# Routed attention and MLP: two raw weight buffers in the memory of the MLP's weight sums, loaded two chunks ahead

## The chip, the cores and the metric

The kernel runs on one core of a Trainium2 chip. A core has five engines that run their own instruction streams[...]: TensorE (PE in the profile; its weight loads are PEld), VectorE (DVE), ScalarE (ACT), GpSimd (POOL) and SyncE (SP), which here does nothing but issue transfers. POOL issues transfers too. The metric is the device time of one launch in microseconds (us); the kernel before was timed three times, and its median is what the change is measured against. The trace is of one further execution.

## The reference, cut to what matters

The inputs are four batches of eight heads, 768 positions and 64 channels. Queries and keys are each assigned to the nearest of 16 centroids of their head; a query sees only the keys of its own cluster. The attention output, with its heads side by side, goes through a layer norm and a two-layer MLP with a residual.

```python
q_assign = np.argmax(np.einsum('bhsd,hcd->bhsc', q_n, c_n), axis=-1)
k_assign = np.argmax(np.einsum('bhsd,hcd->bhsc', k_n, c_n), axis=-1)
mask = q_assign[:, :, :, None] == k_assign[:, :, None, :]
scores = np.where(mask, scale * np.matmul(q, k.transpose(0, 1, 3, 2)), -1000000000.0)
attn = softmax(scores)                       # over the keys
x = (attn @ v), heads side by side           # (4, 768, 512)
xn = (x - mu) / np.sqrt(var + 1e-06) * g_ln
out = x + np.maximum(xn @ w_ch1, 0.0) @ w_ch2   # w_ch1 512x2048, w_ch2 2048x512
```

The two weight matrices arrive as 64-bit floats. [...] the kernel turns them into 32-bit floats itself, in 32 chunks of 128 by 512 numbers (512 KB each as it is loaded), by integer arithmetic on the two 32-bit words of each number.

## The kernel before

The attention stage goes through 16 pairs of heads, n = 0 to 15. Each pair has two slots, one for each half of its queries. The conversion of weight chunks is threaded through this stage: one chunk in each slot of pairs 0 to 6 (14 chunks), one in the first slot only of pairs 7 to 14 (8 chunks). The last 10 chunks are converted in the first part of the MLP.

```python
LOAD AND CONVERSION OF A CHUNK (line numbers of the kernel before)
limit = [NWC, 1]                                                   # 219; [1] is the number of buffers
def load_weight(m):                                                # 229
    if m < NWC and m < limit[0]:
        raw = pools["conv"].tile([P, WC], mybir.dt.int64, tag="raw", name="raw", bufs=limit[1])
        nc.sync.dma_start(out=raw, in_=weight_chunk(m)[0])         # 234, issued by SP
        raws[m] = raw

def split_weight(m):        # reads the high words of raw: three DVE operations, L243, L246, L249
    hi = words[:, :, 1]
    ta = pools["conv"].tile([P, WC], U32, tag="ta", name="ta")
    tb = pools["conv"].tile([P, WC], U32, tag="tb", name="tb", bufs=2)
    ...
def join_weight(m):         # three DVE operations, L258, L262, L263; L263 is the last that reads raw
    ...
    nc.vector.scalar_tensor_tensor(                                # 263
        out=fb, in0=lo, scalar=2.0 ** -52, in1=fb, op0=ALU.mult, op1=ALU.mult)
    nc.gpsimd.dma_start(out=w, in_=fb, accum_op=ALU.add)           # 266, issued by POOL, adds into w
...
TWO SETS OF WEIGHT SUMS, used in the MLP only (tag "ws", two buffers of 4 KB in each partition)
def w1_sums(b, j, which=range(4)):                                 # 592
    if 0 in which:
        t = xpool.tile([P, 4, NDH, P], F32, tag="ws", name="ws", bufs=2)
...
THE ATTENTION STAGE; within an engine the order is that of the code
    load_weight(0)                                                 # 674
    for u in range(len(pairs) * slots):                            # 676
        n, slot = divmod(u, slots)
        if slot == 0 and nxt:
            for side in (1, 0):
                prep_transpose(n + 1, side)       # DVE L275, twice: keys and queries of the next pair
                load(n + 2, "qk"[side])           # SP, four transfers each, rows of 128 bytes
        for i in own: scores(i)                   # PE L392 and ACT exp L388, six steps
        if slot == 0:
            if n and nxt: finish(n - 1, 0)        # PE L453, ACT L461, POOL: flat L463, rdens L464
            if nxt: prep_sims(n + 1)              # PE L297, needs both L275 of this slot
        elif nxt:
            prep_onehot(n + 1)                    # PE L339, needs DVE L324
            prep_mask(n + 1, 0); prep_mask(n + 1, 1)
        if slot and n > 1 and nxt:
            finish(n - 2, 2); finish(n - 2, 3)    # DVE L486 or L490, L498; SP stores x_d L501
        if m is not None: split_weight(m)
        for i in own: weigh(i)                    # PE L404, 12 products
        add_up(n, slot, (0,))                     # DVE L436: sums of four exps
        if slot and n and nxt: finish(n - 1, 1)   # DVE L468, POOL: row L470, rb L478
        if nxt: add_up(n, slot, (1,))             # DVE L439, L441
        if m is not None:
            join_weight(m)
            load_weight(m + 1)                    # SP; waits for L263
        if slot == 0:
            load(n + 1, "v")
            if nxt: prep_turn(n + 1); prep_route(n + 1)   # PE L313; DVE L322, L324
        ...                                       # layer norm of batch 0, from pair 6 on
```

The exps have four buffers of two steps each (tag "e"), of which one slot fills three; the scores have three PSUM buffers.

Of the kernel before, what the change touches and what calls it, by code (L numbers as in the profile page):

```python
# [8 lines left out]
F32 = mybir.dt.float32  # L9
# [10 lines left out]
def kernel(  # L20
# [15 lines left out]
    P = 128  # L36
# [14 lines left out]
    xpool = ctx.enter_context(tc.tile_pool(name="xpool", bufs=1))  # L51
# [4 lines left out]
    def pool(name, bufs, **kw):  # L56
        return stage.enter_context(tc.tile_pool(name=name, bufs=bufs, **kw))
# [4 lines left out]
    conv = pool("conv", 1)  # L62
# [5 lines left out]
    pools = {"t": pool("ps_t", 1, space=PSUM), "conv": conv}  # L68
# [22 lines left out]
    def load(n, names):  # L91
        if n >= len(pairs):
            return
        b, pr = pairs[n]
        for name in names:

            if n and name != "v":
                load_blocks(n, name)
                continue
            shape = [P, 2, NT, D] if name == "v" else [P, NT, 2, D]  # L100
            t = loads.tile(
                shape, F32, tag=name, name=f"{name}_sb", bufs=2 if name == "v" else 1
            )

            parts = 1 if n or name == "v" else NHALF
            for g in range(parts):
                cs = slice(g * NT // parts, (g + 1) * NT // parts)
                for j in range(2):
                    queue = nc.scalar if parts > 1 and j else nc.sync
                    queue.dma_start(  # L110
                        out=t[:, j] if name == "v" else t[:, cs, j, :],
                        in_={"q": q, "k": k, "v": v}[name][b, 2 * pr + j].rearrange(
                            "(p c) d -> p c d", p=P
                        )[:, cs, :],
                    )
            loaded[n][name] = t
# [51 lines left out]
    def norm_centroids(part):  # L168
        if part == 0:
            nc.vector.tensor_tensor(c_sq, c_sb, c_sb, ALU.mult)  # L170
            nc.vector.tensor_reduce(c_ss, c_sq, AX.X, ALU.add)

            nc.vector.tensor_scalar_max(c_ss, c_ss, 2.0 ** -100)
        elif part == 1:
            nc.scalar.activation(c_nrm, c_ss, AF.Sqrt)
        else:

            nc.vector.reciprocal(c_tmp, c_nrm)
            nc.vector.scalar_tensor_tensor(
                out=c_tmp, in0=c_tmp, scalar=c_ss, in1=c_nrm, op0=ALU.mult, op1=ALU.add  # L180
            )
            nc.vector.tensor_scalar(c_nrm, c_tmp, 0.5, 1e-6, op0=ALU.mult, op1=ALU.add)
            nc.vector.reciprocal(c_tmp, c_nrm)
            nc.vector.tensor_scalar_mul(c_sb, c_sb, c_tmp)
# [5 lines left out]
    def turn_centroids():  # L190
        ct_ps = ps("ct_ps")
        nc.tensor.transpose(ct_ps[:D, : H * NCL], c_sb, ident[: H * NCL, : H * NCL])
        ct_v = ct_ps[:D, : H * NCL].rearrange("p (r j c) -> p r j c", j=2, c=NCL)
        for j in range(2):
            nc.vector.tensor_copy(cT[j * D : (j + 1) * D, :, j, :], ct_v[:, :, j, :])
# [10 lines left out]
    NDH, NFH = NDC // 2, NFC // 2  # L206
# [7 lines left out]
    WC = 512  # L214
    NW1 = NDC * FF // WC
    NWC = NW1 + NFC
    raws = {}
    halves = {}
    limit = [NWC, 1]

    def weight_chunk(m):
        if m < NW1:
            o, c = divmod(m, NDC)
            cols = slice(o * WC, (o + 1) * WC)
            return moe_w_ch1[c * P : (c + 1) * P, cols], w1[:, c, cols]
        c = m - NW1
        return moe_w_ch2[c * P : (c + 1) * P, :], w2[:, c, :]

    def load_weight(m):
        if m < NWC and m < limit[0]:  # L230
            raw = pools["conv"].tile(
                [P, WC], mybir.dt.int64, tag="raw", name="raw", bufs=limit[1]
            )
            nc.sync.dma_start(out=raw, in_=weight_chunk(m)[0])
            raws[m] = raw

# [34 lines left out]
    def prep_transpose(n, side):  # L271
        src = loaded[n]["qk"[side]]
        t_sb = prepared[n][side] = heads.tile([P, S], F32, tag=f"t{side}", name=f"t{side}")
        if n:
            nc.vector.transpose(t_sb, src)  # L275
            return
        for g in range(NHALF):
            t = ps_s.tile([P, 2, 512], F32, tag="s", name="qk_ps")[:, 0]
            for c in range(TH):
                nc.tensor.transpose(  # L280
                    t[:, c * P : (c + 1) * P],
                    src[:, g * TH + c, :, :].rearrange("p h d -> p (h d)"),
                    ident,
                )
            if side == 0 or g == 1:
                nc.scalar.copy(t_sb[:, g * HC : (g + 1) * HC], t[:, :HC])
            else:
                nc.vector.tensor_copy(t_sb[:, g * HC : (g + 1) * HC], t[:, :HC])
# [351 lines left out]
    with tc.manual_schedule(engines=order | {mybir.EngineType.SP}):  # L640

        idle = ps_a.tile([P, 512], F32, tag="a", name="idle_ps")

        def busy(m):
            for _ in range(m):
                nc.tensor.matmul(idle[:, :P], zeros, zeros, start=True, stop=True)

        busy(26)
        norm_centroids(0)
        prep_transpose(0, 0)  # L650
        load(1, "q")
        load(0, "v")
        norm_centroids(1)
        norm_centroids(2)
        busy(4)
        prep_transpose(0, 1)
        load(1, "k")
        busy(8)
        turn_centroids()
        busy(8)  # L660
        nc.scalar.activation(warm, warm, AF.Exp, scale=0.0)
        prep_sims(0)
        busy(10)
        prep_turn(0)
        scores(0, "qk", ("qk",))
        prep_route(0)
        prep_onehot(0)
        prep_mask(0, 0)
        prep_mask(0, 1)
        for i in range(1, AHEAD):  # L670
            scores(i, "qk", ("qk",))
        for i in range(AHEAD):
            scores(i, "qk", ("mask", "exp"))
        load_weight(0)
    with tc.manual_schedule(engines=order | {mybir.EngineType.Pool}):
        for u in range(len(pairs) * slots):
            n, slot = divmod(u, slots)
            nxt = n + 1 < len(pairs)
            own = range(GROUP * u, GROUP * (u + 1))
            if slot == 0 and not nxt:  # L680
                finish(n - 1, 0)
            if slot == 0 and nxt:
                for side in (1, 0):
                    prep_transpose(n + 1, side)
                    load(n + 2, "qk"[side])
            for i in own:
                if i >= AHEAD:
                    scores(i)
            if slot == 0:
                if n and nxt:  # L690
                    finish(n - 1, 0)
                if nxt:
                    prep_sims(n + 1)
            elif nxt:
                prep_onehot(n + 1)
                prep_mask(n + 1, 0)
                prep_mask(n + 1, 1)
            for job in extra.pop((n, f"between {slot}"), ()):
                job()
            if slot and n > 1 and nxt:  # L700
                finish(n - 2, 2)
                finish(n - 2, 3)
            m = convert.get((n, slot))
            if m is not None:
                split_weight(m)
            for i in own:
                weigh(i)
            add_up(n, slot, (0,))
            if slot and n and nxt:
                finish(n - 1, 1)  # L710
            if nxt:
                add_up(n, slot, (1,))
            if m is not None:
                join_weight(m)
                load_weight(m + 1)
            if slot == 0:
                load(n + 1, "v")
                if nxt:
                    prep_turn(n + 1)
                    prep_route(n + 1)  # L720
                else:
                    for part in (2, 3):
                        finish(n - 2, part)
                    finish(n - 1, 1)
            elif not nxt:
                for part in (2, 3):
                    finish(n - 1, part)
            for job in extra.pop((n, slot), ()):
                job()
# [25 lines left out]
    hid = pool("hid", 2)  # L755
    rest = ExitStack()
    pools["conv"] = rest.enter_context(tc.tile_pool(name="rest", bufs=1))
    limit[:] = NWC, 2
    for m in range(len(convert), min(len(convert) + 2, NWC)):
        load_weight(m)  # L760

# [440 lines left out]
```

## Time and profile before

| what | value |
|---|---|
| device time, median of 3 | 962.66 us (960.78 to 965.19) |
| span of the traced execution | 957.5 us |
| granted TensorE clock, mean | 0.993 |
| PE busy | 923.3 us, 96% |
| DVE busy | 610.4 us, 64% |
| ACT busy | 345.9 us, 36% |
| POOL busy | 77.4 us, 8% |
| attention stage ends, MLP begins | at about 371 us |
| raw chunks: number, from issue to landing | 32 of 512 KB, median 4.5 us |
| key and query loads | 62 each, 96 KB, median 4.9 and 3.3 us |
| chunk transfers of POOL (w) | 32 of 256 KB, median 5.5 us |

The page has 40 slices of the span of 24 us each, in tenths of busy time. Here the first eight slices of PE read 8 or 9 and the later ones 9 throughout; DVE is at 7 to 9 in the first half and at 2 to 5 after it. The shares of the whole span are therefore averages over stages with different limits: the pairs that convert two chunks, the pairs that convert one, and the MLP. A matmul's end is modelled in the trace, and matmuls overlap, so the elapsed time of a pair of heads is a better measure than PE's busy time in it.

### The profile page before, as it was taken

What the parts mean: (1) busy time and instruction counts of PE and PEld (TensorE: products, weight loads), DVE (VectorE), ACT (ScalarE), POOL (GpSimd) and SP (SyncE); (2) the same over time, 40 slices, a digit from 0 to 9 for tenths busy, and PEclk for the clock granted to TensorE, in tenths of its full rate; (3) what the DMA queues carried; (4) which work ended last, traced back from release to release, by engine and by line L of the source; (5) the groups of instructions that cost most, each with busy time, mean ns of one, the idle gap of its engine ahead of it and who ended that gap; (6) DMA issues with size and microseconds to landing.
All of it is one profiled execution on the core that took longest, in us unless ns stands there. A gap on an engine that the chain in (4) does not pass through costs nothing.

```text
span 957.5 us, 12287 instructions
## 1 busy us (share of the span) xinstructions
PE 923.3 (96%) x4634; PEld 586.5 (61%) x4634; DVE 610.4 (64%) x1050; ACT 345.9 (36%) x545; POOL 77.4 (8%) x145
## 2 busy tenths in 40 slices
PE   8988888899999999999999999999999999999997
PEld 5433333344444444557887556887556888556886
DVE  5778778889979987898883445472345472344431
ACT  4655556566777763332001332000332000433000
POOL 1111111111211121211000000000000000000000
PEclk9999999999999999999999999999999999999999
DMA  7566767799979735655442001121001121000011
GB/s 150 117 132 128 141 139 140 142 192 191 177 157 196 161 68 127 148 134 155 129 156 68 1 1 61 39 83 50 0 1 32 68 83 50 1 1 6 29 43 37
DMA packets 186579, 89.32 MB, mean 93 GB/s; under 512 B 153633, under 2 KB 170129, under 8 KB 186513
## 3 DMA queue, kind: packets, MB, share of 16 engines
q1 hardware_dynamic: 177200, 73.09, 32.3%
q0 software_dynamic: 7712, 14.99, 7.6%
q8 instruction: 38, 0.62, 0.3%
q10 hardware_dynamic: 1600, 0.39, 0.2%
q14 instruction: 29, 0.23, 0.1%
HBM read 62.52 MB, written 17.52 MB: 84 GB/s over the span
## 4 chain that ended last, share of the span: by engine, by line
PE 80%; DVE 11%; DMA 7%; SPq 1%; issue 0%; ACT 0%; DVEq 0%; ACTq 0%
PE x_ps L863 17%; PE x_ps L770 17%; PE z_ps L863 9%; PE s_ps L392 9%; PE z_ps L770 9%; PE a_ps L404 8%; DMA raw<-in_moe_w_ch_dram 7%; PE y_ps L863 4%; PE y_ps L770 4%; DVE two L439 3%; DVE two L436 2%; DVE es L441 1%; DVE tb L263 1%; DVE ta L246 1%; DVE w L258 1%; PE den_ps L453 1%
## 5 line engine op out<-in xcount | busy, mean ns | idle before, releaser
L388 ACT ACTIVATE e<-s_ps 128x768 f32<-128x768 f32 x192 | 152.2, 812 | 23.5 <-PE s_ps L392 21.1
L392 PE MATMUL s_ps<-t,t 64*128 64x384 f32 x768 | 155.1, 483 | 0.0
L404 PE MATMUL a_ps<-e,v_sb 128*64 128x384 f32 x768 | 134.9, 502 | 0.0
L404 PEld LDWEIGHTS a_ps<-e,v_sb 128*64 128x64 f32 x768 | 53.5, 140 | 72.9 <-issue 65.7
L790 DVE TENSOR_TENSOR h<-z_ps,u 128x384 f32<-128x384 f32 x64 | 35.6, 556 | 91.8 <-PE z_ps L770 69.2
L392 PEld LDWEIGHTS s_ps<-t,t 64*128 64x128 f32 x768 | 68.1, 188 | 34.9 <-issue 34.2
L863 PE MATMUL x_ps<-w2t,h 128*128 128x256 f32 x384 | 84.5, 379 | 0.0
L798 ACT ACTIVATE h<-h 128x384 f32<-128x384 f32 x96 | 49.5, 522 | 85.6 <-DVE h L790 85.6
L863 PEld LDWEIGHTS x_ps<-w2t,h 128*128 128x128 f32 x384 | 72.7, 190 | 10.1
L392 PE MATMUL s_ps<-m,mask 64*128 64x384 bf16 x192 | 62.1, 324 | 1.6 <-ACT e L388 1.2
L392 PE MATMUL s_ps<-mask,m 64*128 64x384 bf16 x192 | 61.9, 324 | 0.4 <-DVE mask L362 0.4
L436 DVE TENSOR_TENSOR two<-e 128x1536 f32<-128x1536 f32 x30 | 52.5, 1750 | 8.7 <-ACT e L388 8.7
L785 ACT COPY u<-x_ps 128x384 f32<-128x384 f32 x64 | 30.6, 479 | 75.1 <-PE x_ps L770 75.1
L439 DVE TENSOR_TENSOR two<-two,e 128x1536 f32<-128x1536 f32 x30 | 52.8, 1758 | 1.7
L874 DVE TENSOR_TENSOR o_sb<-x_ps,xb 128x256 f32<-128x256 f32 x48 | 20.0, 417 | 49.6 <-PE x_ps L863 49.6
L785 ACT COPY p<-x_ps 128x384 f32<-128x384 f32 x32 | 15.0, 468 | 96.6 <-PE x_ps L770 96.6
L770 PE MATMUL x_ps<-xn,w 128*128 128x384 f32 x128 | 46.6, 487 | 0.6 <-ACT late L419 0.6
L770 PE MATMUL x_ps<-xt,ws 128*128 128x384 f32 x128 | 46.6, 487 | 0.0
L770 PE MATMUL y_ps<-xn,w 128*128 128x384 f32 x128 | 46.5, 486 | 0.0
L770 PE MATMUL z_ps<-xt,ws 128*128 128x384 f32 x128 | 46.5, 486 | 0.0
L770 PE MATMUL x_ps<-xn,ws 128*128 128x384 f32 x128 | 46.5, 486 | 0.0
L770 PE MATMUL x_ps<-xt,w 128*128 128x384 f32 x128 | 46.5, 486 | 0.0
(146 smaller groups left out, 1401.0 us busy)
## 6 DMA issues: line engine op xcount, KB each, us to landing
raw<-in_moe_w_ch_dram SPq DMA_DIRECT2D x32, 512.0 KB, 4.5
w<-tb POOLq DMA_DIRECT2D x32, 256.0 KB, 5.5
v_sb<-in_v_dram SPq DMA_DIRECT2D x32, 192.0 KB, 4.8
xr<-x_d SPq DMA_DIRECT2D x24, 256.0 KB, 3.5
xb<-x_d SPq DMA_DIRECT2D x48, 128.0 KB, 2.2
out_dram<-o_sb SPq DMA_DIRECT2D x48, 128.0 KB, 1.7
q_sb<-in_q_dram SPq DMA_DIRECT2D x62, 96.0 KB, 3.3
k_sb<-in_k_dram SPq DMA_DIRECT2D x62, 96.0 KB, 4.9
```

Of the source, the lines that this page charges most:

```text
L246: nc.vector.scalar_tensor_tensor(out=ta, in0=hi, scalar=0xC0000000, in1=ta, op0=ALU.bitwise_and, op1=ALU.bitwise_or)
L388: nc.scalar.activation(e, s[:, :, :HC], AF.Exp, scale=SCALE)
L392: nc.tensor.matmul(s[:, j, :HC], of_keys[:, keys], of_queries[:, cols], start=part == first, stop=part != first, skip_group_check=True,)
L404: nc.tensor.matmul(acc[j * D : (j + 1) * D, :HC], loaded[n]["v"][:, j, c, :], e[:, j, :], start=(c == 0), stop=(c == NT - 1),)
L436: nc.vector.tensor_tensor(two, soft.pop(u), soft.pop(u + 1), ALU.add)
L439: nc.vector.tensor_tensor(two, two, soft.pop(u + 2), ALU.add)
L770: nc.tensor.matmul(bank[:, :HC], lhs[:, c, :], rhs[:, c, :], start=first and c == 0, stop=c == NDH - 1, skip_group_check=True,)
L785: nc.scalar.copy(t, bank[:, :HC])
L790: nc.vector.tensor_tensor(h, bank[:, :HC], other, ALU.add)
L798: nc.scalar.activation(h, h, AF.Relu)
L863: nc.tensor.matmul(bank[:, :MH], hidden[lhs + (c,)][:, tt * P : (tt + 1) * P], rhs[:, c, :], start=first and c == 0, stop=c == NFH - 1, sk ...
L874: nc.vector.tensor_tensor(o, bank[:, :MH], x, ALU.add)
```

## The change

The raw chunks of the attention stage no longer have a buffer of their own. They take the two buffers of the tag "ws", which hold sums of MLP weights only from pair 15 on and lie unused before; 128 x 4 x 2 x 128 floats are 4 KB in each partition, exactly one raw chunk. With two buffers a chunk can be loaded while the one before it is still read, so chunks 0 and 1 are loaded ahead of the loop, and the end of chunk m starts the load of chunk m + 2 in place of m + 1. Each load stands where a load stood before in SP's order. The chunks of the MLP keep the two buffers that they had. The aim is to take the load of a chunk out of the time between one chunk and the next.

```diff
-    limit = [NWC, 1]
+    limit = [NWC]
...
     def load_weight(m):
         if m < NWC and m < limit[0]:
-            raw = pools["conv"].tile(
-                [P, WC], mybir.dt.int64, tag="raw", name="raw", bufs=limit[1]
-            )
+            if limit[0] < NWC:
+
+                raw = xpool.tile([P, 4, NDH, P], F32, tag="ws", name="raw", bufs=2)
+                raw = raw.rearrange("p i c f -> p (i c f)").bitcast(mybir.dt.int64)
+            else:
+                raw = pools["conv"].tile([P, WC], mybir.dt.int64, tag="raw", name="raw", bufs=2)
             nc.sync.dma_start(out=raw, in_=weight_chunk(m)[0])
...
         load_weight(0)
+        load_weight(1)
...
                 join_weight(m)
-                load_weight(m + 1)
+                load_weight(m + 2)
...
-    limit[:] = NWC, 2
+    limit[0] = NWC
```

In the loop limit[0] is 22, the number of chunks that the attention stage converts; at the last line it becomes 32. PE, DVE, ACT and POOL have the same instructions in the same order as before; only SP's order differs, in that the second chunk is issued ahead of the loop and the values of pair 1 after the third chunk.

## Prediction

> **What bounds the kernel now.** I read the page's chain of work first. Its shares give PE 80%, DVE 11% and the raw transfer 7%; 7.0% of 957.5 us is 67 us, more than any wait in the list. To see where it lies I took the chain for 60 to 90 us (start, length, what; all in us):
>
> ```profile
> 60.98 0.61 DVE w L258
> ...
> 62.08 0.70 DVE tb L263
> ...
> 62.80 4.39 DMA raw<-in_moe_w_ch_dram
> ...
> 67.21 0.44 DVE ta L243
> ...
> 70.47 1.77 DVE two L439
> 72.27 0.96 DVE es L441
> ...
> 74.32 0.70 DVE tb L263
> ...
> 75.04 4.38 DMA raw<-in_moe_w_ch_dram
> ```
>
> It is a ring of period 75.04 - 62.80 = 12.24 us: the last reader of the buffer ends, the next chunk comes into the same buffer in 4.4 us, and 7.85 us of DVE work ends with that chunk's last reader. PE is not in it. Later, from 204 us, the chain is PE alone. The waits from 19 to 200 us (total, times, longest) confirm that PE follows DVE here:
>
> ```profile
> DVE ta L243 <- DMA raw<-in_moe_w_ch_dram: 37.9, 14, 4.3
> ...
> PEld sim_ps L297 <- DVE t L275: 22.0, 7, 3.4
> PE sim_ps L297 <- DVE t L275: 17.2, 7, 2.7
> ```
>
> DVE idles 37.9 us, less than the chain's 67, since it has transposes or routing to do during part of each transfer. These 14 waits and one of 2.1 us at 14.7 us are all its waits up to 204 us. Then I cut time at the first-slot products of a pair (PE L404), and asked for busy time per pair; columns are elapsed, PE, PEld, DVE, ACT, POOL, clock, DMA share, GB/s:
>
> ```profile
> 65.35:89.88 24.53, 20.57 (x149) 9.47 (x145) 19.91 (x26) 14.45 (x19) 4.54 (x7) 1.00 0.69 132
> 115.15:141.12 25.97, 23.02 (x149) 10.16 (x145) 19.86 (x26) 14.27 (x19) 4.53 (x7) 0.94 0.71 140
> 141.12:166.19 25.07, 21.19 (x150) 9.61 (x146) 19.86 (x26) 14.42 (x19) 4.54 (x7) 1.00 0.73 143
> 214.71:235.03 20.32, 20.32 (x149) 9.57 (x146) 19.53 (x27) 14.45 (x19) 4.43 (x8) 1.00 0.97 196
> ```
>
> Pairs with two chunks last 24.5 to 26.0 us, pairs with one chunk 20.3, with PE full. PE has the same work in both, so 20.32 us is PE's floor for a pair. The question is whether DVE, the transfers and POOL can also do a two-chunk pair in that time.
>
> **What the skill says.** The Trainium skill, "Perfetto Trace Analysis", section "Identifying the Most-Contended Engine", says that a kernel can have regimes with different limits, and that the same gap repeating on an engine can mean too few buffers. The trace agrees: the gap before L243 comes in all 14 slots after the first. "DMA: Bandwidth & Descriptors", "Anatomy of one DMA", says that a semaphore wait is done by the issuing sequencer ahead of the dispatch; so it shows at SP's queue, where the raw load waits 59.0 us in all for L263, and what is queued behind it waits too. "SBUF — State Buffer", "The DMA setup-cost knee", fits a transfer as about 2 us plus bytes over 436 GB/s, an estimate of 3.2 us for 512 KB; the trace has 4.5 (3.7 to 5.8), and I use that. "TensorE: Matmul & The Clock Gate", "What's actually happening", says that an idle TensorE has its clock halved. The trace shows granted clocks of 0.94 and 0.90 in two of the slow pairs, and products of 5.73 and 5.78 us there against 4.09; without pauses these go too.
>
> **The change part by part.** No operation of PE, DVE, ACT or POOL is added, removed or moved. (1) The wait: chunk m + 2 is issued when chunk m is done. From then to its first read lies a slot of DVE work plus the work between two chunks, some 12 us at a pair of 20 us, against 4.5 for the transfer, or 8 with twice the queueing. So I expect all 14 waits to vanish, 37.9 us of DVE idle time.
>
> (2) What DVE then needs. From the transposes at 62.69 to those at 87.22 are 24.53 us, of which 2.69 and 1.48 are waits for raw: 20.36 us back to back. Pairs 0 and 1 lack L490 and L498 and need about 18.5. So DVE needs 20.36 and PE 20.32: as good as equal, with a lead for DVE of nearly 2 us in each of the first two pairs, less the 2.5 us by which it is late at the start (first L436 at 19.95, 0.45 after the first product).
>
> (3) Do the two fit each other in order? I took the PE times of the pair from 214.71 (first product of slot 0, call it 0): simT is there at 4.6, the one-hot transposes of slot 1 are wanted at 9.5, sims of the next pair at 19.6. The fourth exp ends at about -2.1 in slot 0 and 8.7 in slot 1. DVE, if L436 starts at -2.1: both adds, es and the join to 4.2; routing 4.6 to 5.8 (3.7 ahead of its deadline); L490, L498 to 7.7; split to 9.1; adds, reciprocal, es and join to 15.7; transposes to 17.5 (2.1 ahead); split to 18.9; next L436 at 18.9, that is -1.4. It then fills its time, drifts by 0.04 us a pair, and has about 1.5 us left before PE has to wait.
>
> (4) The sum. PE's floor for the first product of slot 1 of pair 7: 29.39 us (slot 1 of pair 0, undelayed) + 7 x 20.32 = 171.6; the trace has it at 204.29. That is 32.7 us, and includes the slow clock. From there on PE is full at 10.4 and 9.9 us for the two slots, then and in the MLP, so what is saved is kept to the end: at most 32.7 us. With DVE and PE equal and no reserve, jitter must cost something: I set 0.3 us a pair, 2 us in all. 962.66 - 32.7 + 2 = about 932 us.
>
> (5) The order of SP: the values of pair 1 go behind the third chunk, so they are issued at about 26 us in place of before 18 us; wanted at about 39, landing takes 4.8. No cost.
>
> **Rivals.** (A) *DVE becomes the bound with waits of its own.* Before, its 4 us of idle time a pair hid whatever came late. Two things come close. The reciprocal L468 needs a round through POOL: row, landing, rb, the chunk's w, flat, landing, rdens, landing. From the traced pairs with one chunk: 0.5 + 5.5 + 1.1 + 0.9 + 0.6 + 5.9 + 0.6 + 5.1 = 20.2 us, my estimate of a ring as long as the pair itself. And tb has two buffers: w of slot 1 is issued by POOL behind rb, at about 19, lands after up to 8.2 at 27.5, and L249 wants the buffer at 29.2. For it: both are tight. Against it: in the 20.3 us pairs L468 has no wait, and there the transfers are as crowded. If DVE waits 1 us a pair in pairs 1 to 6, 6 us less about 1.5 of slack: 936 or 937.
>
> (B) *The DMA engines become the bound.* Their share is 0.71 of 25.27 us in the pair from 89.88, so 18.0 us of work, and 0.89 of 20.32. For it: rows of 128 bytes make most packets (153633 of 186579 under 512 B), and landing grows with load (w from 5.5 to 8.2 us). Against it: shares of 0.97 were sustained at 20.3 us a pair with PE full. If queries or keys came 2 us late in each pair: about 942.
>
> (C) *The wait is hidden anyway,* as when PE would have stood for something else. Against it: PE waits 39 us for L275 in these pairs (two rows above, partly the same time), and only in them. It would leave 955 to 963; I give it little.
>
> **Range and chances.** The floor is 930 and repeats spread by 2 us either way, so the low end is 926. Upwards A and B can give back some 12 us together: high end 944. Faster by over 2% means below 943.4, which needs 19.3 of the 32.7 us; for less, A and B would have to cost over 13 us. I give 0.91, within 2% 0.07, slower by over 2% 0.02: that would take a new wait longer than the old one, and no queue order in the change suggests it.
>
> **What would show it.** Right: no wait of L243 for raw; pairs 1 to 6 at 20.3 to 20.8 us; the first product of slot 1 of pair 7 at 172 to 175 us; clock 1.00 there; the pairs after it and the MLP unchanged in length; DVE busy 19.9 in the two-chunk pairs, hence 96 to 98%. A shows as waits of L468 for rdens or of L249 for w, and PE still waiting for L275 or L324; B as L275 waiting for keys or queries with a DMA share near 0.97. The prediction is wrong if pairs 1 to 6 stay above 22 us, or if the time saved by 172 us is lost again in the one-chunk pairs, where xr, x_d and the statistics now come at the same distance but without DVE's lag.

## The result, and the profile after

| | before | after |
|---|---|---|
| device time, median | 962.47 us (960.78 to 965.19, 4 runs) | 927.29 us (926.83 to 927.98, 4 runs) |
| ratio of after to before, 95% interval | | 0.9632 (0.9609 to 0.9656) |
| span of the traced execution | 957.5 us | 925.0 us |
| mean granted TensorE clock | 0.993 | 0.999 |
| first product of slot 1 of pair 7 | 204.29 us | 171.47 us |
| first product of the MLP | 371.45 us | 338.63 us |

The kernel is faster by 3.7%. In the traces the time is saved by pair 7 (204.29 - 171.47 = 32.8 us) and is kept to the start of the MLP (371.45 - 338.63 = 32.8) and to the end (957.5 - 925.0 = 32.5). Line numbers of the changed kernel are three or four higher than those before: L275 is now L278, L404 is L407, L243 is L246.

The chain of work of the changed kernel, from its page (shares of the span by engine), and then its pieces from 60 to 90 us (start, length, what, in us):

```profile
PE 98%; ACT 0%; DMA 0%; DVE 0%; issue 0%; SPq 0%; ACTq 0%; DVEq 0%
```

```profile
64.57 4.95 PE s_ps L395 x36
69.52 0.44 PE oh_ps L342 x6
69.96 4.02 PE a_ps L407 x24
73.98 4.95 PE s_ps L395 x36
78.93 0.78 PE den_ps L456 x8
79.72 0.65 PE sim_ps L300 x8
80.36 4.05 PE a_ps L407 x24
```

Where the ring of raw transfer and DVE stood, one product of PE follows another; PE's share of the chain went from 80% to 98%. The same stretch in the waits of DVE, from 19 to 172 us (who waited for whom: total us, times, longest):

```profile
DVE two L439 <- ACT e L391: 1.8, 2, 1.6
DVE rdens L471 <- DMA rdens<-flat: 1.1, 1, 1.1
DVE best L325 <- PE simT_ps L316: 0.6, 2, 0.3
```

These are all of them. The 37.9 us for raw are gone, and DVE now waits for exps and for PE: it is ahead of them, not behind. Busy time per pair of heads (same columns as in the prediction), cut again at the first product of each pair's first slot:

```profile
60.00:80.32 20.32, 20.32 (x150) 9.57 (x146) 19.60 (x27) 14.45 (x19) 4.56 (x7) 1.00 0.76 151
100.63:120.94 20.31, 20.31 (x149) 9.57 (x145) 19.78 (x26) 14.45 (x19) 4.65 (x7) 1.00 0.96 175
141.26:161.58 20.32, 20.32 (x150) 9.57 (x146) 19.87 (x27) 14.45 (x19) 4.82 (x7) 1.00 1.05 199
181.89:202.21 20.32, 20.32 (x150) 9.60 (x146) 18.80 (x26) 14.45 (x19) 4.01 (x7) 1.00 0.98 207
```

A two-chunk pair (the first three rows) takes what a one-chunk pair takes (the last), 20.3 us, with DVE at 96 to 98% of it in these rows and the clock at 1.00. In the pair from 120.94 us, not shown, DVE is at 93%, since L471 waited 1.1 us there.

How much room DVE has is read from two instructions in the timeline of the changed kernel (start, length):

```profile
76.15 0.94 DVE L278 STREAM_TRANSPOSE t<-q_sb 128x768 f32<-128x768 f32 x1
```

```profile
79.53 0.83 PE L300 MATMUL sim_ps<-t,cT 128*32 128x384 f32 x8
```

The transposes end at 77.09 and PE wants them at 79.53: 2.4 us of lead. It is the same a pair and two pairs later (97.40 against 99.85, 117.72 against 120.16). After the wait of L471, at 132.71 us, it is 1.4 (139.08 against 140.48).

### The profile page after: what moved, and what is told of

The parts are those of the page before. It is cut to its first block, busy times and chain, and to the rows that moved or that the text cites. A ratio compares the mean times of both kernels' runs of the same rounds, so it can differ in the third digit from the quotient of the medians.

```text
span 925.0 us, 12294 instructions
## 1 busy us (share of the span) xinstructions
PE 913.7 (99%) x4634; PEld 584.9 (63%) x4634; DVE 610.4 (66%) x1050; ACT 346.1 (37%) x545; POOL 77.7 (8%) x145
## 4 chain that ended last, share of the span: by engine, by line
PE 98%; ACT 0%; DMA 0%; DVE 0%; issue 0%; SPq 0%; ACTq 0%; DVEq 0%
PE x_ps L867 18%; PE x_ps L774 18%; PE s_ps L395 17%; PE a_ps L407 14%; PE z_ps L867 9%; PE z_ps L774 9%; PE y_ps L867 4%; PE y_ps L774 4%; PE den_ps L456 1%; PE sim_ps L300 1%; PE simT_ps L316 1%; PE oh_ps L342 1%; DMA k_sb<-in_k_dram 0%; ACT e L391 0%; DVE mask L365 0%
## 5 line engine op out<-in xcount | busy, mean ns | idle before, releaser
L407 PE MATMUL a_ps<-e,v_sb 128*64 128x384 f32 x768 | 130.9, 490 | 0.0
L407 PEld LDWEIGHTS a_ps<-e,v_sb 128*64 128x64 f32 x768 | 52.3, 137 | 69.6 <-issue 58.3
L878 DVE TENSOR_TENSOR o_sb<-x_ps,xb 128x256 f32<-128x256 f32 x48 | 20.1, 418 | 49.1 <-PE x_ps L867 49.1
```

What stands on the lines that cost most here:

```text
L407: nc.tensor.matmul(acc[j * D : (j + 1) * D, :HC], loaded[n]["v"][:, j, c, :], e[:, j, :], start=(c == 0), stop=(c == NT - 1),)
L878: nc.vector.tensor_tensor(o, bank[:, :MH], x, ALU.add)
```

## Experiments

My theory: the time came from a ring of the last read of a raw chunk, the transfer of the next into the same buffer, and the DVE work up to that chunk's last read; PE takes over at its floor once the ring is cut. Rivals: the place in memory matters; the distance of two chunks in the code matters; part of the gain is TensorE's clock; after the change it is DVE, not PE, that sets the time. Ratios are to runs of the kernel before on the same chip.

**One buffer in the memory of the weight sums.** The changed kernel without its second buffer, and so without the load ahead.

```diff
-                raw = xpool.tile([P, 4, NDH, P], F32, tag="ws", name="raw", bufs=2)
-                raw = raw.rearrange(...).bitcast(mybir.dt.int64)
+                if not single:
+                    one = xpool.tile([P, 4, NDH, P], F32, tag="ws", name="raw", bufs=2)
+                    single.append(one.rearrange(...).bitcast(mybir.dt.int64))
+                raw = single[0]
...
-        load_weight(1)
...
-                load_weight(m + 2)
+                load_weight(m + 1)
```

Expected: 

> The raw chunks lie in the memory of the weight sums, but all in one of its two buffers, and each is loaded at the end of the one before. Theory (ring): the ring is back, 962 us plus or minus 3, with 14 waits of about 38 us for raw. Rival (the gain comes from the place in memory, or from the 4 KB that the pool of the conversion no longer takes): 927 to 935 us.

Measured: 960.72 us, ratio 1.0004 (0.9994 to 1.0015). The waits of this run from 17 to 210 us:

```profile
DVE ta L249 <- DMA raw<-in_moe_w_ch_dram: 39.5, 14, 4.1
PEld sim_ps L303 <- DVE t L281: 21.8, 7, 3.4
```

The ring is back as it was. The place in memory has no part in the gain.

**Two buffers, loads asked for one chunk ahead.** The changed kernel without its two lines that load further ahead.

```diff
-        load_weight(1)
...
-                load_weight(m + 2)
+                load_weight(m + 1)
```

Expected: 

> The changed kernel with its two buffers, but nothing loaded ahead of the loop by the code and the end of chunk m followed by the load of chunk m + 1 as before. SP's order is not fixed by the code here, so a load without an unfinished reader can go out early. Theory (the ring of last reader, transfer, first reader was the cost): the second buffer alone breaks the ring, 927 us plus or minus 2. Rival (the two lines that load further ahead are what does it): about 960 us, with waits of L246 for raw in most slots.

Measured: 929.28 us, ratio 0.9684 (0.9651 to 0.9717). The second buffer alone brings nearly all. But three waits for raw, 4.2 us in all, were left in its trace, so I ran it again beside the changed kernel.

Expected: 

> The kernel with two buffers whose loads are asked for one chunk ahead (e1), once more beside the changed kernel. Theory (a load behind keys and queries in SP's queue is late in two or three slots; the trace of e1 had three waits of L246, 4.2 us, of which 1.6 reached PE): 928.5 to 929.5 us, 1.5 to 2 more than the changed kernel. Rival (chance of the first run): the same as the changed kernel within 0.5 us.

Expected of the changed kernel beside it: 

> The changed kernel once more, on the same chip and in the same rounds as the runs beside it, so that differences of 1 to 2 us among the experiments can be read: 927 us plus or minus 1, every theory alike.

Measured: 929.43 us (0.9672; 0.9656 to 0.9687) against 926.43 (0.9641; 0.9626 to 0.9656): 3.0 us apart, and no run of one lies in the range of the other (928.56 to 930.20; 925.90 to 926.84). It is no chance, and larger than I expected. In the trace of the first run the chunk for the second slot of a pair is issued at 126.75 us, behind the eight loads of keys and queries that SP issues from 119.02 on, and DVE starts on it 5.9 us later, after a wait of 2.1 us:

```profile
132.63 0.43 DVE L246 TENSOR_SCALAR ta<-raw 128x512 uint32<-128x512 uint32 x1 [2.13 <-DMA raw<-in_moe_w_ch_dram]
```

In the changed kernel the chunk issued at that place in SP's order (at 126.49 us) is the one for the slot after, so the same delay costs nothing. The chain of work of the second run shows that this is what costs the time. From 65 to 163 us it passes, in each pair, the loads of keys or queries at SP, the raw chunk behind them and DVE; in the changed kernel beside it the chain is PE alone there. One such place:

```profile
82.80 0.66 SPq L83
83.50 6.50 DMA raw<-in_moe_w_ch_dram
90.03 0.44 DVE ta L246
```

So the second chunk of distance pays for the queue at SP ahead of the load.

**One buffer, released early.** The kernel before, with the low words copied out by a fourth operation of the split, and the next load asked for right after it.

```diff
         nc.vector.tensor_single_scalar(tb, hi, 0x7FF00000, op=ALU.bitwise_and)
+        if m < 22:
+            lo = xpool.tile([P, 4, NDH, P], F32, tag="ws", name="lo", bufs=2)
+            lo = lo.rearrange("p i c f -> p (i c f)")[:, :WC]
+            nc.vector.tensor_single_scalar(lo, words[:, :, 0], 2.0 ** -52, op=ALU.mult)
+            raws[m] = lo          # the join reads lo in place of raw
...
                 split_weight(m)
+                load_weight(m + 1)
...
                 join_weight(m)
-                load_weight(m + 1)
```

Expected: 

> The kernel before with its one raw buffer, but a fourth operation of the split (about 0.42 us) copies the low words out, scaled, so that the raw buffer is free right after the split and the next chunk is loaded while DVE adds the exps and joins. Theory (what counts is the time from the last read of a chunk to the first read of the next, not the number of buffers): no wait for raw; DVE then needs 20.36 + 2 x 0.42 = 21.2 us a pair against 20.3 of PE, so with about 2.4 us of lead to use up 2 to 4 us more than the changed kernel: 929 to 931 us. Rival (two buffers are needed): above 950 us.

Measured: 935.95 us, ratio 0.9749 (0.9717 to 0.9782): between the two. Five waits for raw, 8.1 us in all, were left. The timeline of DVE and of SP's issues in this run shows why, for one of them:

```profile
83.24 0.41 DVE L253 TENSOR_SCALAR lo<-raw 128x512 f32<-128x512 uint32 x1
...
94.84 0.43 DVE L243 TENSOR_SCALAR ta<-raw 128x512 uint32<-128x512 uint32 x1 [1.93 <-DMA raw<-in_moe_w_ch_dram]
```

```profile
81.09 3.31 SPq L83 DMA_DIRECT2D k_sb<-in_k_dram  x4
84.50 4.65 SPq L83 DMA_DIRECT2D q_sb<-in_q_dram  x4
89.25 0.59 SPq L234 DMA_DIRECT2D raw<-in_moe_w_ch_dram  x1
```

The buffer is free at 83.65, but SP is still at the loads of keys and queries, which nobody needs for another pair; the raw load goes out 5.6 us late. The last three of the five waits follow such a queue; the first two, at 39.40 and 61.07 us, follow loads of values (v). So I let the raw load go first:

```diff
                 for side in (1, 0):
                     prep_transpose(n + 1, side)
-                    load(n + 2, "qk"[side])
...
                 split_weight(m)
                 load_weight(m + 1)
+            if slot == 0 and nxt:
+                for side in (1, 0):
+                    load(n + 2, "qk"[side])
```

Expected: 

> The kernel with one raw buffer that is released early (e6), with the loads of keys and queries of a first slot asked for after the raw chunk in place of before it, so that most of them stand behind it in SP's queue. In e6 the chunk of a first slot was issued at 89.25 us, 5.6 us after its buffer came free at 83.65, because SP was still at the eight loads of keys and queries ahead of it. Theory (that queue, not the single buffer, gave the waits for raw in e6): hardly any wait for raw (under 2 us in all), and 0.84 us more DVE work a pair as in the run with the doubled operation: 927.5 to 930 us. Rival (with one buffer the time from release to use is too short for the transfer itself): about 935 us, as e6.

Measured: 926.60 us, ratio 0.9643 (0.9626 to 0.9660), beside 926.43 for the changed kernel. The waits of DVE from 17 to 175 us name raw no more:

```profile
DVE t L283 <- DMA k_sb<-in_k_dram: 1.8, 1, 1.8
DVE two L447 <- DVE two L444: 0.5, 1, 0.5
```

One raw buffer is enough, if it is free early and its load does not stand behind others. It saves no memory here: the copied low words take the two buffers of "ws". It was not the number of buffers that cost the time, but that the transfer lay between the last read of one chunk and the first read of the next. The expected cost of the extra operation (0.84 us of DVE a pair) did not come: DVE's lead at the sims falls from 2.0 us (77.62 against 79.62) to 0.15 (160.72 against 160.87), and PE never waits for it.

**TensorE's clock.** The kernel before, with small products in the place where PE waits.

```diff
         sim = ps("sim_ps")
+        if 1 <= n <= 7:
+            for _ in range(24):
+                nc.tensor.matmul(sim[:, :P], identb, identb, start=True, stop=True)
```

Expected: 

> The kernel before, with 24 small bf16 products of 128 columns on PE ahead of the sims of pairs 1 to 7, which run in the time in which PE waits there. They keep TensorE's clock up; the ring of DVE and raw transfers is as before. Theory (the ring passes DVE and the transfer only, so the slow clock of the kernel before cost nothing): 962 us plus or minus 2, with a clock of 1.00 in all pairs. Rival, from my prediction (the slow clock was part of what is saved): 957 to 959 us.

Measured: 962.11 us, ratio 1.0014 (0.9997 to 1.0032). But the clock still fell to 0.93 in one pair, so this said little. A second run had 38 products there and 26 ahead of the one-hot transposes.

Expected: 

> The kernel before with 38 small products ahead of the sims and 26 ahead of the one-hot transposes of pairs 1 to 7, so in both of the places where PE waits for DVE. In the run with 24 at the sims alone the clock still fell to 0.93 in one pair, so that run said little. Theory (the ring passes DVE and the transfer only, the slow clock cost nothing): 961 us plus or minus 2, the clock at 0.99 or more in all pairs from 41 to 190 us. Rival, from my prediction: 957 to 958 us.

Measured: 963.56 us, ratio 1.0032 (1.0018 to 1.0047). Two stretches of this run, and then the same of the kernel before (columns as above):

```profile
90.00:115.00 25.00, 25.00 (x220) 13.22 (x218) 18.81 (x26) 15.34 (x21) 4.37 (x7) 1.00 0.67 132
166.00:192.00 26.00, 25.01 (x212) 13.19 (x209) 20.56 (x28) 14.82 (x20) 4.30 (x7) 1.00 0.76 163
```

```profile
90.00:115.00 25.00, 20.91 (x145) 9.48 (x145) 19.85 (x26) 14.36 (x19) 4.60 (x7) 1.00 0.71 138
166.00:192.00 26.00, 23.31 (x149) 10.14 (x145) 19.85 (x26) 14.52 (x19) 4.57 (x7) 0.90 0.73 149
```

The clock is at 1.00 and no time is won. The chain of work from 19 to 205 us of this run is DVE and the raw transfers alone, and that of the kernel before from 34 to 203 us as well: the slow clock lay beside the ring and cost nothing. In the trace the 3 us lost are in the ring too. The late first product (21.57 us in place of 19.50) is not in the chain; the ring's load at 38.69 us is where it was (38.61), and the 13 transfers from there on take 64.9 us in all in place of 62.0. Why they took longer is not shown. Note the first row: PE is busy for all of 25 us, and yet the time is set by the ring.

**Who sets the time after the change.** First less DVE work: one operation of the join left out for 14 chunks.

```diff
-        nc.vector.tensor_single_scalar(tb, w.bitcast(U32), 0xFF800000, op=ALU.bitwise_and)
+        if m >= 14:
+            nc.vector.tensor_single_scalar(tb, w.bitcast(U32), 0xFF800000, op=ALU.bitwise_and)
```

Expected: 

> The changed kernel with one DVE operation of the join (L265, 0.43 us) left out for the 14 chunks of pairs 0 to 6, so their low words are scaled by a wrong power of two; DVE has 6.0 us less to do. Theory (after the change PE alone sets the time): no change against the changed kernel, 927 us plus or minus 1. Rival (DVE still sets it): about 921 us.

Measured: 926.60 us, ratio 0.9635 (0.9616 to 0.9654); 6 us less of DVE work change nothing (the changed kernel has 0.9632 and 0.9641). Then more of it: the third operation of the split done twice, and four times.

```diff
-        nc.vector.tensor_single_scalar(tb, hi, 0x7FF00000, op=ALU.bitwise_and)
+        for _ in range(2 if m < 14 else 1):      # second run: 4
+            nc.vector.tensor_single_scalar(tb, hi, 0x7FF00000, op=ALU.bitwise_and)
```

Expected, done twice: 

> The changed kernel with the third operation of the split (0.42 us) done twice for the 14 chunks of pairs 0 to 6: 0.84 us more DVE work a pair, 5.9 us in all. Theory (DVE and PE need the same time for a pair; DVE's lead over PE at the sims is 2.45 us in the trace and cannot be won back before pair 7): DVE loses 0.84 us a pair from pair 2 to 6, 5.5 x 0.84 = 4.6, less the lead of 2.4: 929 to 930 us, with waits of PE for L278 from about pair 4 on. Rival (PE alone counts and DVE has room): 927 us. Rival (DVE sets the time fully): 933 us.

Expected, done four times: 

> The same with the operation done four times: 2.5 us more DVE work a pair, 17.6 us in all. Theory: 5.5 to 6.5 pairs x 2.5 = 14 to 16, less the lead of 2.4: 938 to 941 us. Rival (PE alone): 927 us. Rival (DVE fully): 945 us. The difference between this run and the one with the operation done twice is free of the lead: two operations in 14 slots less what falls in pair 0 and 1, 9 to 11 us.

Measured: 927.83 us (ratio 0.9647; 0.9624 to 0.9670) and 941.01 us (0.9785; 0.9762 to 0.9808), on the chip on which the run with less work had 926.60. The first 14 repeats cost 1.2 us, the next 28 cost 13.2. The first is below what I expected (2 to 3), the second above (9 to 11). A repeat takes not 0.42 but 0.46 us of DVE's time: from the start of the operation to the start of the next are 0.34 us in the changed kernel (78.06 to 78.40), 0.81 with the operation doubled (120.75 to 121.56). So the 28 repeats are 12.9 us, and all of them count. For the first 14, the transposes of the run with the operation doubled show why they cost little:

```profile
117.96 0.97 DVE L279 STREAM_TRANSPOSE t<-k_sb 128x768 f32<-128x768 f32 x1
...
138.96 0.97 DVE L279 STREAM_TRANSPOSE t<-k_sb 128x768 f32<-128x768 f32 x1
```

They are 21.00 us apart, without a wait of DVE between them; less the 0.93 added, DVE needs 20.1 us for a pair, not 20.36. The changed kernel shows the same where DVE does not wait for a whole pair: its transposes at 138.14 and 158.22 us are 20.08 apart. So with the operation doubled DVE falls behind PE's 20.31 by 0.69 us a pair and uses up its lead of 2.4 us in three and a half pairs; PE waits for it first at 140.85 us. PE sets the time after the change, with DVE 0.2 us a pair below it.

**More chunks in the attention stage.** If a second chunk costs nothing in pairs 0 to 6, why not in pairs 7 to 14?

```diff
-    TWICE = 7
+    TWICE = 15
```

Expected: 

> The changed kernel with two chunks in each of the pairs 0 to 14, so 30 of the 32 chunks are converted in the attention stage and 2 in the MLP in place of 10. Nothing is left out. Theory: DVE is busy 18.5 to 19.8 us in the one-chunk pairs and gets 3.5 us more, so 22 to 23 us in pairs 7 to 13 where PE needs 20.3: 12 to 18 us lost, and nothing won in the MLP, where PE was full: 938 to 945 us. Rival (the waits of DVE for exps leave room, or the MLP profits from 8 chunks less): 925 to 930 us.

Measured: 933.79 us, ratio 0.9709 (0.9687 to 0.9732): 7.2 us slower than the run with less DVE work beside it, so a loss as expected, but half the size. Two of its pairs:

```profile
203.51:225.54 22.03, 20.50 (x150) 9.47 (x146) 21.48 (x31) 14.45 (x19) 4.88 (x8) 1.00 1.00 194
246.77:267.54 20.77, 20.50 (x150) 9.47 (x146) 20.32 (x27) 14.51 (x19) 4.80 (x8) 1.00 1.01 220
```

In the seven pairs from 182.03 to 332.74 us DVE has no wait at all; they take 150.71 us, against 143.10 for the same pairs of the changed kernel (181.89 to 324.99). So DVE is the bound there, as I said, but with less work. The six operations of a chunk take 3.2 us in a row (split 77.01 to 78.40, join 73.47 to 75.26 in the changed kernel's timeline), not 3.5; and the seven pairs of the changed kernel have 125.57 us of DVE work, among them one pair with 17.0 and one with 15.8, where I had reckoned with 18.5 to 19.8 in each. 125.57 + 7 x 3.2 = 148.0 is close to the DVE busy time of this run (147.19). The MLP has 8 chunks less to convert and is shorter by 0.7 us only: 932.1 - 341.71 us of span after the last pair's second products, against 925.0 - 333.96. There PE was full before.

## Why the prediction was right, and where it was off

I said 932 us, 926 to 944; it is 927.29. The mechanism and the place of the gain were as predicted; the size was 4.7 us too small. The result is even below the floor of 930 that I named, and inside the range only because its low end, 926, lies 4 us below that floor.

- **What bounds the kernel.** The ring was read rightly, but not for the reason that I gave first: the 67 us of raw transfers are not more than any wait in the list. ACT waited 96.6 us in all for products of the MLP (L785 for L770), and that is not in the chain. What singles the transfer out is that it lies in the chain of work.
- **The wait (step 1).** All 14 waits for raw are gone. The prediction read the repeating gap with the Trainium skill, "Perfetto Trace Analysis" (there in the section "Optimization Strategy"), as a possible sign of too few buffers; the runs narrow this, since one raw buffer, released early, gives 926.60 us. The transfers landed in 5.3 us (median), 7.4 at most, well inside the 12 us that I reckoned.
- **DVE's need (step 2).** 20.36 us a pair was too high by 0.3: the doubled operation and the changed kernel give 20.1. "As good as equal" to PE was nearly right, but on the side that does no harm: a lead is not used up, and after L471's wait it grew again by 0.2 us in a pair.
- **The fit (step 3).** I put the transposes 2.1 us ahead of the sims and expected a drift that leaves 1.5; in the trace they are 2.4 ahead for three pairs, 1.4 after L471's wait and 1.6 a pair later (159.15 against 160.79). No wait of PE for DVE from 19 us to the MLP was left.
- **The sum (step 4).** This step was off, in two terms that make up the 4.7 us. The floor itself was not: 171.6 us predicted for slot 1 of pair 7, 171.47 in the trace. The 2 us for jitter did not come. And I took 32.7 us, measured in one trace of the kernel before, off the median of three timed runs; that traced execution had taken 959.28 us, 3.4 less than the median of 962.66. From the traced execution the sum is right: 959.28 - 32.7 = 926.6, and the traced execution of the changed kernel took 926.89. The three runs were on the high side: 31 later runs of the kernel before, all on one chip, have a median of 960.23 and spread from 957.12 to 963.69 us, the changed one over 1.2 us in its four. The trace of the kernel with one buffer in the other memory has 39.5 us of waits for raw in place of 37.9. That the spread of the kernel before comes from its 14 transfers on the ring fits this, but is only argued.
- **The clock.** My sum said that the gain "includes the slow clock". That is wrong in its reason: with the clock held at 1.00 the kernel before did not get faster. The time was lost to the ring, and the slow products ran beside it.
- **SP's order (step 5).** No cost, as predicted: the products of pair 1 begin at 39.69 us with no wait.
- **Rival A** was close, as I had it: L471 waits 1.1 us for rdens once in these pairs and 1.2 in pair 7, and tb never made DVE wait. The lead swallowed it. **Rival B**: the DMA share rose to 0.96 and 1.05 in single pairs, and neither keys nor queries came late after the first pair. **Rival C** is refuted by the result.

## What to carry to other kernels

Look for a ring in the chain of work: the last reader of a buffer, the transfer into it, the work up to its next last reader. Its period is the sum of the three (in the trace before, 4.39 + 7.85 = 12.24 us) whatever the engines' busy shares are, and it is cut by getting the transfer out of it: a second buffer, or the one buffer released earlier. Then find the next floor before promising a gain, here PE's 20.32 us a pair from stages without the ring, and check how close the other engines come to it. Look also at what stands in front of the load in its issuing queue: behind eight loads that nobody needs yet an early release lost some 9 of 34 us here.

## What I had not expected of the hardware

The order in one issuing queue was worth some 9 of the 34 us won: with one buffer released early, 935.95 us (ratio 0.9749) with the raw load behind the loads of keys and queries, 926.60 (0.9643) with most of them behind it. Four such loads of 96 KB in rows of 128 bytes kept SP's queue for 2.7 to 7.5 us in these traces (2.69 us at 16.86 and 7.48 at 160.11 in the changed kernel), against a median of 0.35 us for the issue of a raw chunk of 512 KB. And a run in which PE is busy for every microsecond of a stretch, at full clock, was no faster than the one with the gaps (963.56 against 960.50 us).
